# A new form for the state update, a later place for the routing's ranks, and new priorities

## The chip, the cores and the metric

The program runs on one core of a Trainium2 chip. The core has TensorE (PE, with its weight loads PEld), VectorE (DVE), ScalarE (ACT) and GpSimd (POOL); SyncE (SP) issues most DMAs. Each engine works through its own instructions in the order in which the program holds them, and waits on semaphores for the others. The metric is the device time of one execution. Before the change it is 979.59 us, the median of three runs (979.5 to 981.68).

## The reference

Three layers follow each other over 3072 tokens of 384 numbers.

```python
# 1. delta rule, 4 batches x 8 heads, 768 steps, head_dim 48
for t in range(S):
    y[:, :, t] = einsum('bhd,bhde->bhe', q[:, :, t], state)
    v_old = einsum('bhde,bhd->bhe', state, kt)
    state = state + bt[...] * einsum('bhd,bhe->bhde', kt, vt - v_old)
# 2. gated dense layer, 384 -> 1536 -> 384
x = ((x @ w_a) * (x @ w_b)) @ w_out
# 3. eight experts, one for each token, 384 -> 1024 -> 384
e_idx = argmax(x @ w_gate + modality_bias[modality_id], axis=1)
out[mask] = gate_w[mask, None] * (maximum(x[mask] @ w1[e], 0) @ w2[e])
```

## The kernel before

**Number format.** A product of float32 operands is made of float16 pieces: each operand is split into a high half and the low rest, and three matmuls add hi*hi, hi*lo and lo*hi into one region of PSUM. So nearly every operand has a copy by ACT (hi) and a subtraction by DVE or POOL (lo).

**Delta rule.** The 768 steps are cut into 6 chunks of 128. A group g = 4*c + b is chunk c of batch b; there are 24. Within a chunk a triangular system is solved on DVE (L648, L653) and by block products (m1 to m4); from one chunk to the next a state of 48 x 48 per head is carried. For a group, s1_mm takes the state into the right-hand side, s2_mm applies the inverse, s3_mm makes the output and s4_mm the new state: 8 heads, three matmuls each, hi*hi, hi*lo and lo*hi, with 48 key columns as weight and the result on 48 partitions of one PSUM tile, at 0 for an even b and at 64 for an odd one (L905 to L909). s4_f (L915) adds it to the state in float32, s4_hi and s4_lo split that again for the next chunk. The keys' tile t1 holds for a head the hi half in columns 0 to 47 and the lo half in 64 to 111 of 128, with padding between; 20 groups have a state update (the last chunk needs none).

**Dense layer.** The tokens go in tiles t of 256 (the first one in two halves, t = -2 and -1), each in 12 steps m over the 1536 hidden columns: f_mm (18 matmuls into pab, L362 to L364), f_a (ACT copies a), f_ab (DVE multiplies by b), f_hi (ACT, the hi half of g), f_lo (L384, the lo half of g, on DVE or POOL), o_mm (L395 to L397, three matmuls for each half tile into po). Two steps behind f_mm comes o_mm. There are two buffers a, freed by f_lo, and five buffers g.

**Routing.** When the 12 steps of tile t are done, the two PSUM banks po of the tile hold 256 rows of output with 8 logits. r_lg (DVE, L416 to L422) takes logits, argmax and one-hot rows oh; r_mx (DVE, L429) reads both banks for a row maximum; r_hi (ACT, L438) and r_lo (DVE, L444) split the rows; r_rk (PE, L461 to L465) multiplies the one-hot rows by a triangle of ones and writes each token's rank among its expert's tokens into a spare corner of the tile's first bank; r_po (DVE) turns it into a position, and r_sc (POOL) scatters the rows there. setup_routing (L167 to L192) makes the constants for this once, on POOL: it fills a zero tile z, writes pads with it, loads the modality numbers md and builds the bias.

**Experts.** z_cal (DVE, L1158 to L1245) works out which 128-row slots belong to which expert; for each slot h_mm makes pH (L1290 to L1292), DVE subtracts hl (L1303), g_mm and a scatter follow. The first slots' work stands among the last dense steps.

**Order.** Every step is declared with do(f, args, engine, cost, priority, after, take): the steps it comes after and the buffers it takes and who frees them. emit() (L213) then plays a list scheduler: on each engine it takes, among the steps that could start within PATIENCE of the earliest, the one with the least start + HURRY x priority, and it writes the program in the order of its model's starts. The table TUNE adds a number to each priority, by step name and phase of the program; the table ENGINE says where a step runs. Semaphores come from the reads and writes of the tiles: what the planner doesn't know, the engine still waits for on the chip. r_rk is such a case: it is declared after r_lg alone, but the program makes it wait for the other readers of its bank.

## Time and profile before

| | |
|---|---|
| Median of three runs | 979.59 us |
| Profiled execution | 978.26 us, span 976.5, mean granted clock 0.943 |
| PE busy | 879.6 us, 12156 matmuls |
| DVE, ACT, POOL busy | 716.9, 540.4, 281.7 us |
| DMA | 163.57 MB, 167 GB/s |

The span is the stretch from the first to the last instruction that the profile holds; the profiled execution's own time is 1.8 us longer. Busy time is what an engine spends in instructions; for PE it is a union of overlapping matmuls, so that the number of starts per microsecond says more than a row's length. In a row of a timeline the first number is the start, the second the length, and the brackets at its end hold the idle time ahead of it and what ended it. The granted clock is a share of full speed.

### The profile page before, as it was taken

To read this page: it belongs to the slowest core of one execution; us is meant where nothing else is said; L and a number is where in the kernel's file an instruction comes from. 1 tells how busy PE (TensorE), PEld (TensorE's weight loads), DVE (VectorE), ACT (ScalarE), POOL (GpSimd) and SP (SyncE) were. 2 spreads that over 40 slices of the span, in tenths; PEclk is the share of its full clock that TensorE was granted. 3 is DMA by queue.
4 is the path that set the end of the run, shared out by engine and by line. 5 is a ranking of instruction groups with operands and counts; after the bars stand their busy time and mean duration, and the time that the engine had idled before them with its cause. 6 is when DMAs were issued, how large, how long until landed. Compare 5 with 4: busy or idle time off the path is not lost. (4 is left out here: it accounts for less than half of the span.)

```text
span 976.5 us, 30822 instructions
## 1 busy us (share of the span) xinstructions
PE 879.6 (90%) x12156; PEld 704.0 (72%) x12156; DVE 716.9 (73%) x1751; ACT 540.4 (55%) x1072; POOL 281.7 (29%) x409
## 2 busy tenths in 40 slices
PE   3665568999999999999999999999999799999996
PEld 1433367888778887878788887788787677777774
DVE  7889787857997799679975888545877955555551
ACT  4543465547655565555755564555566745555551
POOL 4521015223331233212430422021134423333331
PEclk9676569999999999999999999999999999999998
DMA  7896688674669483864775543331588987999980
GB/s 206 247 245 185 167 175 208 140 181 78 143 150 202 78 130 102 183 152 88 146 173 122 114 88 100 61 64 35 167 249 218 336 256 234 260 264 261 257 218 19
DMA packets 266498, 163.57 MB, mean 167 GB/s; under 512 B 188221, under 2 KB 245357, under 8 KB 266352
## 3 DMA queue, kind: packets, MB, share of 16 engines
q1 hardware_dynamic: 262720, 150.27, 63.9%
q0 software_dynamic: 3632, 11.29, 3.4%
q8 instruction: 100, 1.64, 0.7%
q14 instruction: 46, 0.38, 0.1%
HBM read 97.10 MB, written 30.31 MB: 130 GB/s over the span
## 5 line engine op out<-in xcount | busy, mean ns | idle before, releaser
L332 DVE SCALAR_TENSOR_TENSOR w1l<-w1f,w1h 128x1024 f16<-128x1024 f32 x69 | 80.7, 1220 | 67.2 <-ACT w1h L329 59.5
L362 PE MATMUL pab<-xt,wa 128*128 128x256 f16 (+1 forms) x468 | 122.5, 267 | 2.7 <-DVE a L374 1.3
L364 PE MATMUL pab<-xt,wa 128*128 128x256 f16 (+1 forms) x468 | 122.4, 266 | 0.0
L363 PE MATMUL pab<-xt,wa 128*128 128x256 f16 (+1 forms) x468 | 122.4, 266 | 0.0
L362 PE MATMUL pab<-xt,wb 128*128 128x256 f16 (+1 forms) x468 | 122.3, 266 | 0.0
L363 PE MATMUL pab<-xt,wb 128*128 128x256 f16 (+1 forms) x468 | 122.3, 266 | 0.0
L364 PE MATMUL pab<-xt,wb 128*128 128x256 f16 (+1 forms) x468 | 122.2, 266 | 0.0
L374 DVE SCALAR_TENSOR_TENSOR a<-pab,a 128x256 f32<-128x256 f32 (+1 forms) x156 | 62.2, 400 | 70.0 <-ACT a L329 68.4
L329 ACT ACTIVATE a<-pab 128x256 f32<-128x256 f32 (+1 forms) x156 | 56.5, 364 | 94.2 <-PE pab L364 82.8
L397 PE MATMUL po<-wo,g 128*128 128x392 f16 x288 | 94.8, 329 | 1.7 <-POOL g L384 1.7
L395 PE MATMUL po<-wo,g 128*128 128x392 f16 x288 | 95.1, 330 | 0.0
L396 PE MATMUL po<-wo,g 128*128 128x392 f16 x288 | 94.7, 329 | 0.0
L1290 PE MATMUL pH<-xg_t,w1h 128*128 128x128 f16 x504 | 85.4, 219 | 4.0 <-DMA xg_t<-w2f 3.8
L1292 PE MATMUL pH<-xg_t,w1l 128*128 128x128 f16 x504 | 85.4, 219 | 0.0
L1291 PE MATMUL pH<-xg_t,w1h 128*128 128x128 f16 x504 | 85.4, 219 | 0.0
L329 ACT ACTIVATE g<-a 128x256 f16<-128x256 f32 (+1 forms) x156 | 61.3, 395 | 41.6 <-DVE a L374 32.3
L329 ACT ACTIVATE w1h<-w1f 128x1024 f16<-128x1024 f32 x69 | 68.5, 1047 | 3.7 <-DMA w1f<-in_moe_w_dram 3.2
L648 DVE TENSOR_TENSOR tmp<-A,T 128x31 f32<-128x31 f32 (+15 forms) x186 | 68.4, 368 | 1.5
L653 DVE TENSOR_TENSOR T<-T,tmp 128x31 f32<-128x31 f32 (+15 forms) x186 | 66.3, 357 | 1.7
L762 POOL TENSOR_TENSOR tl<-ttf,th 128x1024 f16<-128x1024 f32 x19 | 42.8, 2256 | 83.7 <-ACT th L329 82.2
L1313 PE MATMUL po<-w2h,hh 128*128 x200 | 65.2, 326 | 1.3 <-ACT hh L1297 0.8
L1315 PE MATMUL po<-w2h,hl 128*128 x200 | 65.2, 326 | 0.0
(301 smaller groups left out, 2863.2 us busy)
## 6 DMA issues: line engine op xcount, KB each, us to landing
w1f<-in_moe_w_dram SPq DMA_DIRECT2D x69, 512.0 KB
w2f<-in_moe_w_dram SPq DMA_DIRECT2D x32, 384.0 KB
gsc<-gs SPq DMA_DIRECT2D x22, 512.0 KB
bq<-aq SPq DMA_DIRECT2D x48, 128.0 KB
bk<-ak SPq DMA_DIRECT2D x40, 128.0 KB
qt<-in_q_dram SPq DMA_DIRECT2D x24, 192.0 KB
kt<-in_k_dram SPq DMA_DIRECT2D x24, 192.0 KB
raw<-in_moe_w_a_dram SPq DMA_DIRECT2D x12, 384.0 KB
```

The source lines that it names most:

```text
L329: S_.activation(out=out, in_=in_, func=ACTF.Copy, scale=scale)
L332: V.scalar_tensor_tensor(out=out, in0=in_, scalar=scale, in1=hi, op0=ALU.mult, op1=ALU.subtract)
L362: T_.matmul(out=p[:, i], lhsT=wa[i][0][:, kk, sl], rhs=xt[:, kk], start=(kk == 0), stop=False)
L363: T_.matmul(out=p[:, i], lhsT=wa[i][0][:, kk, sl], rhs=xt[:, KD + kk], start=False, stop=False)
L364: T_.matmul(out=p[:, i], lhsT=wa[i][1][:, kk, sl], rhs=xt[:, kk], start=False, stop=(kk == KD - 1))
L395: T_.matmul(out=po, lhsT=g[:, 0, sl], rhs=wo[0][:, m], start=(m == 0), stop=False)
L396: T_.matmul(out=po, lhsT=g[:, 0, sl], rhs=wo[1][:, m], start=False, stop=False)
L397: T_.matmul(out=po, lhsT=g[:, 1, sl], rhs=wo[0][:, m], start=False, stop=(m == KF - 1))
L648: V.tensor_tensor(out=LN[c, 2], in0=A[:, j + 1 : 32, j : j + 1].to_broadcast([128, n, w]), in1=T[:, j : j + 1, 0:w].to_broadcast([128, n, ...
L1290: T_.matmul(out=pH[:, u], lhsT=wh[kk][:, sl], rhs=xt[:, kk], start=(kk == 0), stop=False)
L1291: T_.matmul(out=pH[:, u], lhsT=wh[kk][:, sl], rhs=xt[:, KD + kk], start=False, stop=False)
L1292: T_.matmul(out=pH[:, u], lhsT=wl[kk][:, sl], rhs=xt[:, kk], start=False, stop=(kk == KD - 1))
```

## The change

It has four parts.

1. r_rk writes into the second bank of its tile instead of the first; for the last tile (t = 11) it has a tile of its own. The planner now holds r_rk back until r_mx, r_hi and r_lo of that bank are planned.
2. s4_mm takes all 128 columns of a head's keys (hi, padding, lo) as one weight, and multiplies it by uh and by ul: two matmuls per head instead of three. The result has the hi keys' part on partitions 0 to 47 and the lo keys' part on 64 to 111, so a second addition, s4_g, adds the second part to the state behind s4_f. (The lo*lo product is in the sum now.)
3. All numbers of TUNE, PATIENCE and HURRY are new; one line of TUNE is shown.
4. In ENGINE, f_lo goes to POOL in phase 4 (tiles 2 to 10) and to DVE in phase 9; s4_lo goes to DVE everywhere; some a_sq go to POOL, some a_ev, a_lo and p_lo to DVE, c_g2 and x_ev to ACT.

```diff
-    "f_lo:4": 264.09, "f_lo:9": -565.7, "f_mm:3": 234.1, "f_mm:4": 7667.22, "f_mm:9": -249.21, "g_ev:9": -77.5, "g_mm:9": -155.1, "g_sc:9": 43.1,
+    "f_lo:4": -0.4463, "f_lo:9": 310.7308, "f_mm:3": 941.7648, "f_mm:4": 6328.6844, "f_mm:9": 425.6198, "g_ev:9": -1393.6713, "g_mm:9": 1749.0876,
...
-    "c_lo:3": "DVE", "f_lo:3": "POOL", "f_lo:4": "DVE", "f_lo:9": "POOL", "k_pad:0": "DVE", "k_pad:1": "POOL", "m_lo:1": "DVE", "m_lo:2": "POOL",
+    "c_lo:3": "DVE", "f_lo:3": "POOL", "f_lo:4": "POOL", "f_lo:9": "DVE", "k_pad:0": "DVE", "k_pad:1": "POOL", "m_lo:1": "DVE", "m_lo:2": "POOL",
...
-        R["pr"] = pr = PO[2 * t][:, WO : WO + 3 * E].rearrange("p (i e) -> p i e", e=E)
+        if t == NG // 2 - 1:
+            pr = ps_ab.tile([128, 3 * E], F32, name="pr", tag="ab")
+        else:
+            pr = PO[2 * t + 1][:, WO : WO + 3 * E]
+        R["pr"] = pr = pr.rearrange("p (i e) -> p i e", e=E)
...
-        o = 64 * (b % 2)
         for h in range(H):
-            T_.matmul(out=pS[o : o + 48, h], lhsT=t1[:, h, 0, 0:D], rhs=uh[:, h], start=True, stop=False)
-            T_.matmul(out=pS[o : o + 48, h], lhsT=t1[:, h, 0, 0:D], rhs=ul[:, h], start=False, stop=False)
-            T_.matmul(out=pS[o : o + 48, h], lhsT=t1[:, h, 1, 0:D], rhs=uh[:, h], start=False, stop=True)
+            for u in (uh, ul):
+                T_.matmul(out=pS[:, h], lhsT=t1[:, h].rearrange("p t d -> p (t d)"), rhs=u[:, h], start=(u is uh), stop=(u is ul))
...
-        o = 64 * (b % 2)
-        V.scalar_tensor_tensor(out=Sf[b], in0=PS.pop((g, 4))[o : o + 48], scalar=2.0**-6, in1=Sf[b], op0=ALU.mult, op1=ALU.add)
+        V.scalar_tensor_tensor(out=Sf[b], in0=PS[g, 4][0:48], scalar=2.0**-6, in1=Sf[b], op0=ALU.mult, op1=ALU.add)
+
+    def s4_g(g):
+        b = g % B
+        V.scalar_tensor_tensor(out=Sf[b], in0=PS.pop((g, 4))[64:112], scalar=2.0**-6, in1=Sf[b], op0=ALU.mult, op1=ALU.add)
...
-            do(s4_hi, (g,), "ACT", 0.41, o + 5.6, after=[(s4_f, g), (s3_mm, g)])
+            do(s4_g, (g,), "DVE", 0.47, o + 5.55, after=[(s4_f, g)])
+            do(s4_hi, (g,), "ACT", 0.41, o + 5.6, after=[(s4_g, g), (s3_mm, g)])
...
-        do(r_rk, (t,), "PE", 0.1, o + 0.1, after=[(r_lg, t)])
+        if last:
+            do(r_rk, (t,), "PE", 0.1, o + 0.1, after=[(r_lg, t)], take=[("ps_ab", 2, [(r_po, t)])])
+        else:
+            do(r_rk, (t,), "PE", 0.1, o + 0.4, after=[(r_lg, t), (r_mx, t), (r_hi, gs[1]), (r_lo, gs[1])])
```

PE around the ranks' product of tile 9, before: po_11945 and po_11949 are the tile's two banks, pab_12885 is one dense step's tile of 18 matmuls, oh the one-hot rows.

```order
L397 MATMUL po_11949<-wo0_89,g_12817 128x392
L362 LDWEIGHTS wa0_85
L362 MATMUL pab_12885<-xt_12184,wa0_85 128x256
...
L364 MATMUL pab_12885<-xt_12184,wb1_88 128x256
L461 LDWEIGHTS tri_94
L461 MATMUL po_11945<-oh_12908,tri_94 128x8
...
L465 MATMUL po_11945<-oh_12908,ones_95 128x8
L362 LDWEIGHTS wa0_85
```

PE at the same place now: the bank is po_12047, the tile's second one, and pab_12720, pab_12763 and pab_12799 are three dense steps.

```order
L404 MATMUL po_12047<-wo0_89,g_12699 128x392
L369 LDWEIGHTS wa0_85
L369 MATMUL pab_12720<-xt_12038,wa0_85 128x256
...
L369 MATMUL pab_12763<-xt_12038,wa0_85 128x256
...
L369 MATMUL pab_12799<-xt_12038,wa0_85 128x256
...
L371 MATMUL pab_12799<-xt_12038,wb1_88 128x256
L472 LDWEIGHTS tri_94
L472 MATMUL po_12047<-oh_12743,tri_94 128x8
...
L476 MATMUL po_12047<-oh_12743,ones_95 128x8
```

Before, one dense step stands between the tile's last output matmul and the ranks' product; now three do, and the product writes into the bank that the last output matmul wrote.

POOL at the routing's set-up, before (g is what f_lo writes, tri, offc and tok the set-up's constants, pl a step of the delta rule):

```order
L384 TENSOR_TENSOR g<-a,g 128x128 x2
L404 TENSOR_SCALAR sl<-my 128x1
L405 TENSOR_TENSOR sl<-sl 128x1
L384 TENSOR_TENSOR g<-a,g 128x128
L169 AFFINE_SELECT tri<-ones 128x128
L170 IOTA iota_97 128x8
...
L192 TENSOR_TENSOR bias<-bias,bt 128x192
L384 TENSOR_TENSOR g<-a,g 128x128 x2
L807 TENSOR_TENSOR pl<-pm,ph 128x512
```

POOL there now (sq is a step that squares keys for a later chunk):

```order
L391 TENSOR_TENSOR g<-a,g 128x128 x2
L411 TENSOR_SCALAR sl<-my 128x1
L412 TENSOR_TENSOR sl<-sl 128x1
L391 TENSOR_TENSOR g<-a,g 128x128 x2
L818 TENSOR_TENSOR pl<-pm,ph 128x512
L391 TENSOR_TENSOR g<-a,g 128x128 x2
L176 AFFINE_SELECT tri<-ones 128x128
...
L199 TENSOR_TENSOR bias<-bias,bt 128x192
L545 TENSOR_TENSOR sq<-kt 128x384
L391 TENSOR_TENSOR g<-a,g 128x128 x2
```

Three f_lo's stood ahead of the set-up, and two directly behind it; now six stand ahead, and a squaring stands between it and the seventh. On PE, c_g3 of the last weight tile, which frees the set-up's buffer, has moved from ahead of the fourth dense step of the first half tile to ahead of the ninth.

DVE at the handover to the experts, before (hl belongs to the experts' first slots, pi is r_po's last, cn to nu are z_cal, w1l and w2l corrections of expert weights):

```order
L444 SCALAR_TENSOR_TENSOR row<-po,io,row 128x384 x2
L1303 SCALAR_TENSOR_TENSOR hl<-pH,hh 128x512 x2
...
L477 CAST pi<-pf 128x2
L332 SCALAR_TENSOR_TENSOR w2l<-w2f,w2h 128x768
L1158 TENSOR_TENSOR cn_14276<-off,offc 1x8
...
L1245 CAST nu<-cum_14283 1x1
L332 SCALAR_TENSOR_TENSOR w1l<-w1f,w1h 128x1024 x5
L1303 SCALAR_TENSOR_TENSOR hl<-pH,hh 128x512 x2
L332 SCALAR_TENSOR_TENSOR w2l<-w2f,w2h 128x768 x2
```

DVE there now:

```order
L488 CAST pi<-pf 128x2
L451 SCALAR_TENSOR_TENSOR row<-po,io,row 128x384
L1170 TENSOR_TENSOR cn_14022<-off,offc 1x8
...
L1257 CAST nu<-cum_14029 1x1
L1315 SCALAR_TENSOR_TENSOR hl<-pH,hh 128x512 x2
L339 SCALAR_TENSOR_TENSOR w1l<-w1f,w1h 128x1024 x2
L451 SCALAR_TENSOR_TENSOR row<-po,io,row 128x384
L339 SCALAR_TENSOR_TENSOR w1l<-w1f,w1h 128x1024
L339 SCALAR_TENSOR_TENSOR w2l<-w2f,w2h 128x768
L1315 SCALAR_TENSOR_TENSOR hl<-pH,hh 128x512
```

r_po and z_cal have moved ahead of the first two hl and of one r_lo; behind z_cal the first hl come at once, and three w1l and w2l corrections, not five, and one r_lo stand ahead of the next one.

## Rows read from the trace of the kernel before

**Rows 1.** the page's first part: busy us and share of the span.
```profile
PE 879.6 (90%) x12156; PEld 704.0 (72%) x12156; DVE 716.9 (73%) x1751; ACT 540.4 (55%) x1072; POOL 281.7 (29%) x409
```

**Rows 2.** windows: stretch, length, busy us by engine, granted clock, DMA share, GB/s.
```profile
0.00:175.00 175.00, 108.02 (x1287) 78.86 (x1288) 142.57 (x348) 88.22 (x185) 51.74 (x84) 0.72 0.81 203
175.00:750.00 575.00, 564.82 (x8446) 462.80 (x8444) 445.99 (x1226) 336.66 (x732) 162.30 (x249) 1.00 0.58 130
750.00:775.00 25.00, 18.58 (x218) 15.02 (x217) 23.66 (x66) 17.37 (x25) 8.87 (x11) 0.94 1.00 308
```

**Rows 3.** PE's timeline at a state update; its loads before 175 us.
```profile
237.26 0.18 PE L879 MATMUL py<-uh,pl 128*128 128x48 f16 x1
237.38 0.20 PE L907 MATMUL pS<-uh,t1k 128*48 128x48 f16 x1
...
237.98 0.18 PE L909 MATMUL pS<-uh,t1k 128*48 128x48 f16 x1
238.09 0.34 PE L395 MATMUL po<-wo,g 128*128 128x392 f16 x1
...
L907 PEld LDWEIGHTS <-t1k x16: 99/108/130, 138.4 to 159.7; 128*48 128x48 f16 x16
```

**Rows 4.** PE's timeline, the state's first product and a dense step.
```profile
242.63 0.20 PE L822 MATMUL pk<-sst,ak 128*128 128x48 f16 x1
...
243.04 0.27 PE L362 MATMUL pab<-xt,wa 128*128 128x256 f16 x1
243.15 0.27 PE L363 MATMUL pab<-xt,wa 128*128 128x256 f16 x1
```

**Rows 5.** groups of DVE: the addition to the state (count, busy us, mean ns).
```profile
L915 DVE SCALAR_TENSOR_TENSOR sf<-pS,sf 48x384 f32<-48x384 f32 x20 | 11.0, 550 | 0.5
```

**Rows 6.** groups by shape: f_lo on DVE and POOL, its product.
```profile
L384 DVE TENSOR_TENSOR g<-a,g 128x256 f16<-128x256 f32 x104 | 44.4, 428 | 14.4 <-ACT g L329 14.2
L384 POOL TENSOR_TENSOR g<-a,g 128x256 f16<-128x256 f32 x28 | 23.3, 837 | 45.5 <-ACT g L329 45.4
...
L397 PE MATMUL po<-wo,g 128*128 128x392 f16 x288 | 94.8, 329 | 1.7 <-POOL g L384 1.7
```

**Rows 7.** group of PE: the ranks' product, idle before it, releasers.
```profile
L461 PE MATMUL po<-oh,tri 128*128 128x8 f16 x12 | 2.0, 167 | 6.8 <-DVE mo L429 4.3 <-DVE row L444 1.2 <-DVE oh L422 1.1
```

**Rows 8.** timeline of DVE behind the last output product, routing.
```profile
753.92 0.23 DVE L416 SCALAR_TENSOR_TENSOR lg<-po,sl,bias 128x8 f32<-128x8 f32 x1 [0.27 <-PE po L397]
...
757.85 1.14 DVE L444 SCALAR_TENSOR_TENSOR row<-po,io,row 128x384 f16<-128x384 f32 x2
```

**Rows 9.** timeline of POOL, the routing's set-up.
```profile
152.82 0.42 POOL L175 MEMSET z<- 128x386 f32 x1
...
165.31 0.59 POOL L192 TENSOR_TENSOR bias<-bias,bt 128x192 f32<-128x192 f32 x1
```

**Rows 10.** windows of 4 us around the set-up (columns as in rows 2).
```profile
156.00:160.00 4.00, 2.61 (x57) 2.28 (x54) 2.97 (x7) 3.40 (x9) 0.56 (x2) 1.00 1.03 340
164.00:168.00 4.00, 2.33 (x28) 1.62 (x26) 0.80 (x3) 2.02 (x5) 3.70 (x6) 1.00 1.07 219
168.00:172.00 4.00, 4.00 (x39) 3.69 (x37) 3.54 (x7) 2.31 (x7) 1.54 (x2) 0.51 0.36 67
```

**Rows 11.** timeline of ACT, its stall at 129 us.
```profile
129.07 0.55 ACT L329 ACTIVATE wa<-raw 128x384 f16<-128x384 f32 x1 [5.16 <-DVE raw L963]
```

**Rows 12.** handover: timeline of DVE, then what PE waited for, 740 to 800.
```profile
758.90 1.28 DVE L1303 SCALAR_TENSOR_TENSOR hl<-pH,hh 128x512 f16<-128x512 f32 x2
...
761.73 0.15 DVE L1158 TENSOR_TENSOR cn<-off,offc 1x8 f32<-1x8 f32 x1
...
766.43 5.74 DVE L332 SCALAR_TENSOR_TENSOR w1l<-w1f,w1h 128x1024 f16<-128x1024 f32 x5
...
PE pH L1290 <- DVE hl L1303: 5.0, 2, 4.2
```

**Rows 13.** waits of POOL, 240 to 740 us (total, times, longest).
```profile
POOL nm L449 <- DVE mx L418: 59.0, 5, 23.0
```

More of the change, by code (lines that the diff above doesn't have):

```diff
@@ L25 @@
 TUNE = {
[53 rows of a table removed]
[60 rows of a table added]
 }
 PHASE = 25.3
-PATIENCE = ({'PE': 0.7054, 'ACT': 0.1823, 'DVE': 0.06, 'POOL': 0.0334, 'SP': 0.0142}, {'PE': 0.0192, 'ACT': 0.0784, 'DVE': 0.0625, 'POOL': 0.1252, 'SP': 0.6242})
-HURRY = ({'PE': 0.0067, 'ACT': 0.1015, 'DVE': 0.1386, 'POOL': 0.9737, 'SP': 0.0345}, {'PE': 0.7037, 'ACT': 4.3321, 'DVE': 0.2391, 'POOL': 0.9527, 'SP': 0.8016})
+PATIENCE = ({'PE': 0.1441423, 'ACT': 0.0531199, 'DVE': 0.0137721, 'POOL': 2.8466535, 'SP': 0.0044223}, {'PE': 0.0382268, 'ACT': 0.0401974, 'DVE': 0.0662866, 'POOL': 0.0645055, 'SP': 0.8143324})
+HURRY = ({'PE': 0.2337259, 'ACT': 3.7188375, 'DVE': 0.2014005, 'POOL': 0.7865635, 'SP': 1.4968712}, {'PE': 0.0884019, 'ACT': 0.0543269, 'DVE': 0.0452602, 'POOL': 0.1058564, 'SP': 0.0275992})
 WLEAD = 14.0
@@ L1433 @@
         if c < C - 1:
-            do(s4_mm, (g,), "PE", 0.6, o + 5.2, after=[(s2_lo, g), (s3_mm, g)], take=[("pss", 2, [(s4_f, g)])])
+            do(s4_mm, (g,), "PE", 0.4, o + 5.2, after=[(s2_lo, g), (s3_mm, g)], take=[("pss", 2, [(s4_f, g), (s4_g, g)])])
             do(s4_f, (g,), "DVE", 0.47, o + 5.5, after=[(s4_mm, g)] + ([(k_st, b)] if c == 0 else []) + ([(k_st, b - 1)] if c == 0 and b % 2 else []))
-            do(s4_hi, (g,), "ACT", 0.41, o + 5.6, after=[(s4_f, g), (s3_mm, g)])
+            do(s4_g, (g,), "DVE", 0.47, o + 5.55, after=[(s4_f, g)])
+            do(s4_hi, (g,), "ACT", 0.41, o + 5.6, after=[(s4_g, g), (s3_mm, g)])
             do(s4_lo, (g,), "POOL", 0.87, o + 5.7, after=[(s4_hi, g)])
```

121 rows, old and new, of tables (ENGINE, TUNE) are left out of this document.

## The prediction

> **What bounds the kernel now.** I read the page first, for the engine that is never idle. PE is busy 879.6 of 976.5 us [rows 1], so 97 us of idle PE is all that a change of order can win; more needs less work on PE. The windows say where that idle time lies [rows 2]: 67 us in the first 175 us, 10.2 in the 575 us behind them, 6.4 in the 25 us from 750 to 775, and the other 13 in the experts' 200 us and their tail. At the start no engine is full and DVE comes nearest (142.6 of 175): the start is a web of waits, with the granted clock at 0.72 on average. From 175 us on the granted clock is 1.00, PE is 98% busy, and DVE, ACT and POOL all have slack. So there are three kinds of place: the middle, where a microsecond less on PE is a microsecond gained; the handover at 750, where the routing's last steps hold PE; and the start, where what counts is who waits for whom. The chain of waits says nothing here (two pieces of the last write).
>
> The sum is made against the profiled execution, 978.26 us, 1.3 below the median of 979.59. Both are the same program, so I take the difference over to the median.
>
> **1. The state update: -7.2 us.** Twenty groups of 24 matmuls become twenty of 16. I read the price in starts, because the 0.18 us that a row shows is depth, not pitch. The last matmul ahead of a group starts at 237.26, the group's first at 237.38, its last at 237.98, the next product at 238.09 [rows 3]: 0.83 us from start to start, of which 0.60 is 24 matmuls at some 0.025, and the rest the way into the 128*48 shape (0.12) and out of it (0.11), where neighbours of one shape start 0.025 apart (0.60 / 24). The new group has the form of the state's first product, 16 matmuls of a 128*128 shape and 48 columns, two to a weight: 242.63 to 243.04, 0.41 us [rows 4]; with 0.025 for the entry, 0.43. So a group saves 0.40 us. Two of the twenty lie before 175 us, where PE waits anyway (16 of its first line, eight to a group [rows 3]), so 18 count: 7.2. Bounds: 8.0 if all twenty count; 3.6 if only the eight matmuls go (18 x 8 x 0.025) and the shape change isn't what costs the 0.2. I take 7.2, since the gaps stand at both ends of the group and at none inside.
>
> The Trainium skill says in "TensorEngine Tiling (Array Packing)", Key Properties, that changing the tiling mode drains the engine; the trace agrees, with the 0.12 and 0.11 us above, and the change takes that drain away wherever the neighbours are 128*128. Its page "TensorE: Matmul & The Clock Gate", section LDWEIGHTS, speaks against the change: a load takes as long as it has columns (P / 1.2 ns, an estimate of 40 ns for 48 and 107 ns for 128). The trace differs: pairs with 128-column weights also start 0.025 us apart [rows 4].
>
> The second addition on DVE (s4_g) costs 20 x 0.55 = 11 us of DVE [rows 5]. DVE is busy 446 of 575 us in the middle [rows 2], and the 90 subtractions f_lo that leave it take 90 x 0.43 = 38 us away [rows 6]. I cost it at nothing; if its cover is gone, it is up to 0.55 us later per group on the way to the next chunk's state, which is needed many microseconds later.
>
> **2. The wait at the ranks' product: -5.5 us.** PE stood idle 6.8 us in all at its 12 first matmuls, mostly until the row maximum was read from the same bank [rows 7]. The order after an output product is on DVE: the second logits are taken at 753.92, and r_lo's two end at 757.85 + 1.14 = 758.99 [rows 8], so a product that waits for the last reader is free 5 us after the output. In the order before, one step of 18 matmuls of 0.11 us, 2 us [rows 4], was often all that stood between; now three such steps stand there for the tile that I show, and for the others 4 to 16 us by the same count. Only t = 10 has less than 5 us (36 matmuls, 4 us), so I leave 1.2 there and take 6.8 - 1.2 = 5.6, rounded to 5.5. For the last t the product has a bank of its own and only needs the one-hot rows. Bounds: 6.8 (all of it goes) and 2 (DVE is late by another 2 us in half of the places, since all four steps of DVE and ACT must now be over). What is late next is r_po: 45 to 157 rows of PE lie between the ranks' product and the next output product, so it is covered.
>
> **3. f_lo of the middle on POOL: 0.** 90 subtractions go from DVE to POOL, at 0.84 instead of 0.43 us each [rows 6]. Each stands between ACT's copy g and the third matmul of an output product; 90 x 0.41 = 37 us is what it would cost if nothing lay between, 0 if the product always comes later. The trace bears out the second: 28 of the wide ones were on POOL already, and of all 288 rows of that matmul only one waited for POOL, 1.7 us in the start [rows 6]. POOL is busy 162 of 575 us [rows 2], so 75 us more fit. I take 0, with 0 to +17 as the range (below).
>
> **4. The routing's set-up on POOL: +4 us.** From its first MEMSET to its last addition setup_routing holds POOL from 152.82 to 165.31 + 0.59 = 165.9, 13.1 us [rows 9], a wait for its own load included; that MEMSET writes a staging buffer, which comes free with c_g3 of the last weight tile, on PE. In the new order that PE step comes some 12 us of PE's work later and six f_lo's stand ahead of the set-up, so it runs from about 165 to 179, and one a_sq and the seventh f_lo are queued behind it. PE has about 9 us of steps between c_g3 and the output product that needs the seventh, by the order and the pitches above: two f_mm of half width (1 us each), five o_mm of half width (0.5, scaled by columns), s2, s3 and s4 (24, 40 and 16 matmuls of 0.025, 2 us) and six short ones (2 to 3). The set-up takes 13.1 and the two behind it over 1: a wait of 5 to 6. Before, PE stood idle 4 - 2.61 = 1.39 us around 158 and 1.67 around 166, with the set-up on POOL, and then the granted clock was 0.51, the lower of its two levels (1.2 of 2.4 GHz), for 4 us [rows 10]. The half clock may come again behind the new wait, or not. So +2.5 by the waits alone, +6 with a longer stretch of half clock; DVE's longer queue before the first tiles adds up to 3, and ACT's stall of 5.16 us that ends at 129 us [rows 11] partly goes, since the new order has m4_a ahead. I take +4, between 0 and +9.
>
> **5. The handover: -0.8 us.** After the last output product PE waits 25 - 18.58 = 6.4 us [rows 2], 4.2 of it for the subtraction hl, which DVE does behind z_cal (from 761.73, 4.7 us) and five weight corrections of 5.74 us together [rows 12]. Now one r_lo, two hl and one correction of w2 no longer stand ahead of z_cal, which ends some 2.8 us earlier (0.57 + 1.28 + almost 1), but the first two hl come behind it: they end at 766.4 - 2.8 + 1.3 = 764.9 instead of 760.2, so PE waits some 5 us there. The second pair has three corrections ahead of it, not five, and the 4.2 is mostly gone. In all 6.4 becomes some 5.6. Bounds: -3, and +3.4 if the weight corrections moved behind them make the fourth or fifth slot late.
>
> **The sum.** -7.2 - 5.5 + 0 + 4 - 0.8 = -9.5 us: 968.8 against the profiled execution, 970 against the median.
>
> **Rivals.**
> *A. The start takes it all back.* Term 4 at its upper end, +9, with term 2 at 4 and term 1 at 6: -6 - 4 + 9 - 0.8 = -1.8, so 978, give or take 2. For it: the start holds 67 of 97 us of idle time and every wait there has lowered the clock. Against it: the same stretch had waits before, and ACT's stall shortens.
> *B. POOL becomes the late one (slower).* f_lo shares POOL's strict order with r_nm, which waited 59 us for DVE in five places [rows 13], and with indirect writes. Where one of these stands ahead of an f_lo, the buffer a isn't freed, the next products have no place to go, and PE stops. From 1.4 us per tile over nine tiles (12.6 us), with term 4 at +6, the gain is gone: -7.2 - 5.5 + 12.6 + 6 - 0.8 = +5, 985. For it: POOL waited for DVE in these rows before. Against it: 28 f_lo's caused no wait there, and five buffers g lie between.
> *C. The change doesn't do what it says.* The shape change costs nothing by itself and the ranks wait on, because DVE is as late as before: -3.6 - 2 + 4 - 0.8 = -2.4, 977. Against it: rows 3 and the moved rows.
> *D. The wide weight is paid.* If a pair cost the 0.1 us that one load lasts [rows 3], a group of 16 would take 1.6 us and not 0.43, 0.77 more than the group before (0.83): 20 x 0.77 - 5.5 + 4 - 0.8 = +13, 993. Against it: the pitch in rows 4. The rule of the skill named above would have this sign.
>
> **How the numbers follow.** The forecast (964 to 975) has 0.55, A 0.16, B 0.13, C 0.08, D 0.02, and 0.06 is for a start that gets shorter, 955 to 963. What a measurement can tell from no change is 0.3%, 2.9 us: below 976.7 and above 982.5. Faster: 0.55 + 0.06 + a quarter of A and a third of C, 0.68. Slower: B, D and an eighth of A, 0.17. The rest is 0.15. The range leaves out half of B, D and the best starts: 961 to 984.
>
> **What would show it.** Term 1: the state update's groups at x160 with two lines' worth of matmuls, 0.41 us from first start to the next one, shape 128*128. Term 2: idle ahead of the ranks' product under 1.5 us. Term 3: no new wait of PE for POOL in 175 to 750, whose busy sum falls by some 5 us. Term 4: POOL's set-up ending near 180, and PE waiting 5 us for g there; I am wrong if 175 us of the old start become more than 184. Term 5: 750 to 775 with one long wait instead of the last one. If PE is idle in the middle for over 15 us, B is true.

## The result, and the profile after

The changed kernel takes 989.07 us (median), the kernel before 979.55 beside it: a ratio of 1.008, with a 95% interval from 1.0053 to 1.0106, so 0.8% or 9.5 us slower. Forecast were 970, and 961 to 984 as the range. The profiled execution took 988.83 us with a span of 986.7, against 978.26 and 976.5. Of all executions behind the ratios below one is left out, which took 1752 us where the eleven others of its kernel took 978 to 985.

The page's first part and the windows of [rows 1, 2], of the changed kernel (columns as there):

```profile
PE 874.6 (89%) x11996; PEld 700.9 (71%) x11996; DVE 718.9 (73%) x1687; ACT 544.6 (55%) x1072; POOL 330.2 (33%) x493
```

```profile
0.00:175.00 175.00, 106.27 (x1336) 79.78 (x1336) 148.82 (x364) 92.98 (x188) 48.53 (x74) 0.76 0.81 203
175.00:750.00 575.00, 559.62 (x8245) 456.86 (x8246) 439.62 (x1144) 333.97 (x725) 219.42 (x343) 1.00 0.57 128
750.00:775.00 25.00, 18.64 (x214) 15.95 (x213) 21.56 (x63) 14.84 (x21) 4.89 (x10) 0.86 0.88 305
```

PE has 5 us less to do, and its busy time from 175 to 750 us fell by those 5 us, 564.8 to 559.6, as I had asked for. But they became idle time: idle PE in these 575 us went from 10.2 to 15.4 us. DVE did not become free either (446.0 to 439.6): the second addition came, and the steps of the triangular system became longer. Groups of the changed kernel by shape (count, busy us, mean ns, idle ahead), and then two groups of the triangular system, from the page before (L648, L653) and from the page now (L659, L664):

```profile
L472 PE MATMUL po<-oh,tri 128*128 128x8 f16 x11 | 1.9, 171 | 2.7 <-DVE row L451 2.7
L472 PE MATMUL pr<-oh,tri 128*128 128x8 f16 x1 | 0.2, 169 | 0.0
...
L923 DVE SCALAR_TENSOR_TENSOR sf<-pS,sf 48x384 f32<-48x384 f32 x20 | 10.9, 546 | 1.1 <-PE pS L918 0.7
L927 DVE SCALAR_TENSOR_TENSOR sf<-pS,sf 48x384 f32<-48x384 f32 x20 | 11.2, 560 | 0.6
...
L391 POOL TENSOR_TENSOR g<-a,g 128x256 f16<-128x256 f32 x118 | 89.0, 756 | 197.4 <-ACT g L336 195.3 <-DVE iy L358 1.5
```

```profile
L648 DVE TENSOR_TENSOR tmp<-A,T 128x31 f32<-128x31 f32 (+15 forms) x186 | 68.4, 368 | 1.5
L653 DVE TENSOR_TENSOR T<-T,tmp 128x31 f32<-128x31 f32 (+15 forms) x186 | 66.3, 357 | 1.7
```

```profile
L659 DVE TENSOR_TENSOR tmp<-A,T 128x31 f32<-128x31 f32 (+15 forms) x186 | 81.9, 440 | 2.7
L664 DVE TENSOR_TENSOR T<-T,tmp 128x31 f32<-128x31 f32 (+15 forms) x186 | 73.9, 397 | 2.7
```

For the group of [rows 3] term 1 is exact: the timeline now reads 0.02 us into the group and 0.02 out of it, 0.42 us in all instead of 0.83. Not every group has neighbours of the same shape: where a 32*32 or 64*64 product stands beside it, some 0.5 to 0.6 us remain.

```profile
238.39 0.18 PE L890 MATMUL py<-uh,pl 128*128 128x48 f16 x1
238.41 0.18 PE L918 MATMUL pS<-uh,t1k 128*128 128x48 f16 x1
...
238.79 0.18 PE L918 MATMUL pS<-ul,t1k 128*128 128x48 f16 x1
238.81 0.33 PE L402 MATMUL po<-wo,g 128*128 128x392 f16 x1
```

Of term 2, 4.1 us are there: 2.7 us of idle time against the 6.8 of [rows 7]. What came in its place in the middle, among PE's waits from 200 to 752 us (us in total, times, longest):

```profile
PE py L886 <- DVE ul L339: 4.2, 6, 1.4
PE po L472 <- DVE row L451: 2.7, 2, 2.5
PE pab L369 <- DVE a L381: 2.6, 4, 1.8
```

The first is the low half ul that s3_mm needs, the second the ranks' product, the third the buffer pab that f_ab frees. In the same stretch before they stood at 2.2, 6.0 and 0.2.

Then the experts. The first expert product starts at 752.1 us, 1.6 us earlier than before (753.7), and from there this execution loses all that it loses. Windows from the first product of expert slot 0 to that of slot 8, and on to slot 24, before and then after:

```profile
753.70:822.60 68.90, 62.15 (x751) 50.09 (x749) 48.49 (x91) 38.96 (x53) 22.46 (x25) 0.98 0.87 278
822.60:955.40 132.80, 128.73 (x1536) 101.44 (x1537) 75.12 (x80) 71.92 (x96) 41.64 (x48) 1.00 0.90 247
```

```profile
752.10:831.30 79.20, 65.30 (x750) 53.07 (x749) 53.30 (x96) 42.59 (x58) 17.68 (x25) 0.94 0.88 272
831.30:966.30 135.00, 129.27 (x1539) 101.41 (x1537) 75.25 (x80) 72.08 (x96) 41.64 (x48) 1.00 0.88 237
```

Eight slots take 79.2 us instead of 68.9. Of the 10.3 us, 7.1 are idle PE (13.9 us, 6.8 before) and 3.1 longer busy time, at a granted clock of 0.94 instead of 0.98: it stands at the lower of its two levels, 0.50, from 760.9 to 767.7 us and from 822.4 to 825.8, beside the two long waits below, and before the change only from 772.2 to 775.6. From slot 8 on the pace is the same within 2%: 135.0 and 132.8 us. PE's waits in the 79 us, and the stretch of DVE that answers to [rows 12] (xg_t are a slot's tokens; their rows are fetched into w2f, the four staging buffers that the second weights use too, and transposed from there):

```profile
PE pH L1302 <- DVE hl L1315: 6.3, 2, 5.7
PE pH L1302 <- DMA xg_t<-w2f: 4.3, 1, 4.3
PE po L1326 <- DVE w2l L339: 2.3, 2, 1.6
```

```profile
756.65 0.14 DVE L1170 TENSOR_TENSOR cn<-off,offc 1x8 f32<-1x8 f32 x1
...
761.31 0.13 DVE L1257 CAST nu<-cum 1x1 int32<-1x1 f32 x1
761.37 1.26 DVE L1315 SCALAR_TENSOR_TENSOR hl<-pH,hh 128x512 f16<-128x512 f32 x2
```

The counting z_cal (cn to nu, 756.65 to 761.44) now stands ahead of hl, as the order said, and PE waits 5.7 us for hl. 4.3 us come at 821.8 us, where slot 7 waits for its tokens, and 2.3 for corrections of the second weights (w2l). On DVE 21 of these corrections now stand ahead of the last tile's routing; before the change 26 did. On SP seven of the 32 loads of second weights, 384 KB each, are issued behind the first expert product, the last at 800.0 us; before the change two were, the last at 761.9. By the windows 272 x 79.2 = 21.5 MB instead of 278 x 68.9 = 19.2 MB are moved beside these slots (GB/s by us), and those five loads are 2.0 of the 2.3 MB. In the 50 us ahead, DMA had time for them: its share was 0.69 from 700 to 725 us and 0.65 from there to the first product, against 0.90 and 0.74 before.

### The profile page after: what moved, and what is told of

It reads as the page before. It is cut to its first block, busy times and chain, and to the rows that moved or that the text cites. A ratio compares the mean times of both kernels' runs of the same rounds, so it can differ in the third digit from the quotient of the medians.

```text
span 986.7 us, 30518 instructions
## 1 busy us (share of the span) xinstructions
PE 874.6 (89%) x11996; PEld 700.9 (71%) x11996; DVE 718.9 (73%) x1687; ACT 544.6 (55%) x1072; POOL 330.2 (33%) x493
## 5 line engine op out<-in xcount | busy, mean ns | idle before, releaser
L391 POOL TENSOR_TENSOR g<-a,g 128x256 f16<-128x256 f32 (+1 forms) x142 | 100.8, 712 | 219.9 <-ACT g L336 217.8
L381 DVE SCALAR_TENSOR_TENSOR a<-pab,a 128x256 f32<-128x256 f32 (+1 forms) x156 | 62.1, 400 | 71.3 <-ACT a L336 70.4
L1302 PE MATMUL pH<-xg_t,w1h 128*128 128x128 f16 x504 | 87.0, 221 | 9.5 <-DMA xg_t<-w2f 9.4
L1303 PE MATMUL pH<-xg_t,w1h 128*128 128x128 f16 x504 | 87.0, 221 | 0.0
L659 DVE TENSOR_TENSOR tmp<-A,T 128x31 f32<-128x31 f32 (+15 forms) x186 | 81.9, 440 | 2.7
L664 DVE TENSOR_TENSOR T<-T,tmp 128x31 f32<-128x31 f32 (+15 forms) x186 | 73.9, 397 | 2.7
L1326 PE MATMUL po<-w2l,hh 128*128 x200 | 65.1, 326 | 2.3 <-DVE w2l L339 2.3
```

The source lines that it names most:

```text
L391: eng_of(f_lo, t, m).tensor_tensor(out=g[:, 1], in0=FA.pop((t, m)), in1=g[:, 0], op=ALU.subtract)
L659: V.tensor_tensor(out=LN[c, 2], in0=A[:, j + 1 : 32, j : j + 1].to_broadcast([128, n, w]), in1=T[:, j : j + 1, 0:w].to_broadcast([128, n, ...
L1302: T_.matmul(out=pH[:, u], lhsT=wh[kk][:, sl], rhs=xt[:, kk], start=(kk == 0), stop=False)
L1303: T_.matmul(out=pH[:, u], lhsT=wh[kk][:, sl], rhs=xt[:, KD + kk], start=False, stop=False)
```

## The experiments

Ratios are against the kernel before, run beside them on the same chip, with their 95% intervals.

**One part at a time.** The state product of the change in the kernel before, in an order that is the same instruction by instruction but for it:

```diff
-            T_.matmul(out=pS[o : o + 48, h], lhsT=t1[:, h, 0, 0:D], rhs=uh[:, h], start=True, stop=False)
...
+            for u in (uh, ul):
+                T_.matmul(out=pS[:, h], lhsT=t1[:, h].rearrange("p t d -> p (t d)"), rhs=u[:, h], start=(u is uh), stop=(u is ul))
...
+        for o in (0, 64):
+            V.scalar_tensor_tensor(out=Sf[b], in0=pS[o : o + 48], scalar=2.0**-6, in1=Sf[b], op0=ALU.mult, op1=ALU.add)
```

> The kernel before with the new state update alone: two matmuls per head, 128 key columns as one weight, and the second addition directly behind the first on DVE. Every step stands where it stood. Theory (the form saves what I read from the starts, and the loss comes from elsewhere): 7 us faster than before, 972 to 974, the group 0.43 us from start to start and no new wait. Rival 1 (only the eight matmuls go, the shape change costs nothing): 3.6 us faster. Rival 2 (the saving is used up by the second addition, which makes the next state late): no change, with new waits ahead of the state's first product.

Measured: 988.78 us against 980.77, 1.0091 (1.0061 to 1.012), 8 us slower, worse than the theory and both rivals. A group between 128*128 products saves its 0.40 us, the mean of the 18 behind 175 us 0.35 (0.86 to 0.50). PE's idle time from 200 us to the first expert product grows by more, from 10.0 to 19.7 us. Its waits from 200 to 764 us, of which the first two were 4.3 and 2.2 us before:

```profile
PE po L461 <- DVE mo L429: 5.9, 8, 1.9
PE py L875 <- DVE ul L332: 4.9, 4, 1.6
PE pu L853 <- POOL tl L762: 1.2, 1, 1.2
```

So the term of 7.2 us is a loss when it stands alone. Its two sides were then taken apart. The new form without the second addition (`for o in (0,)`):

> The kernel before with the new state update's 16 matmuls, and without the second addition: the lo keys' part of the product is computed and left out of the state. Every step stands where it stood. Theory (the second addition on DVE, 20 x 0.55 us, is what made the new form slower, because DVE's order in the middle has no slack where PE waits for it): 6 to 8 us faster than the kernel before, 972 to 975. Rival (the wide weight or the result on 112 partitions costs something itself): no faster than before, 980 or more.

Measured: 981.48 us, 1.0007 (0.9982 to 1.0032). Seven us less on PE bring nothing that can be told from noise: PE is idle for 14.9 us from 175 to 750 us instead of 10.2. The rival (the wide weight costs something itself) has no support, since the groups are as short as with the second addition, 0.50 us in the mean. And the kernel before with a second, idle addition on DVE, 20 x 0.55 us:

```diff
+        for s in (2.0**-6, 0.0):
+            V.scalar_tensor_tensor(out=Sf[b], in0=pS, scalar=s, in1=Sf[b], op0=ALU.mult, op1=ALU.add)
```

> The kernel before with its own state update, and one more addition of the same size on DVE behind s4_f (it adds the same product times zero): 20 x 0.55 us of DVE and nothing else. Theory (DVE has no slack at these places): 11 to 16 us slower than before, 991 to 997, the idle time of PE ahead of py, of po and of the ranks' product grown between 200 and 620 us. Rival (DVE has slack, 78% busy): within 3 us of before.

Measured: 987.74 us, 1.0087 (1.0056 to 1.0118), 6.8 us slower than the 980.91 beside it, for this group of DVE:

```profile
L917 DVE SCALAR_TENSOR_TENSOR sf<-pS,sf 48x384 f32<-48x384 f32 x40 | 22.1, 553 | 1.1
```

So 11 us more on an engine that is busy 446 of 575 us [rows 2] cost 7, between theory and rival. The reverse, with no addition at all:

```diff
-        V.scalar_tensor_tensor(out=Sf[b], in0=PS.pop((g, 4))[o : o + 48], ...)
+        PS.pop((g, 4))
```

> The kernel before, without its 20 state additions (s4_f, 48 x 384, 550 ns each, 11.0 us of VectorE); the state is then not updated, and nothing else is changed, the order included. Theory (VectorE's in-order chain sets the pace of the middle, as the idle addition, +11 us of work for +6.8 us, had it): about 6 to 7 us faster, 973 to 974 against 980. Rival (TensorE sets the pace and the idle addition only pushed VectorE over a brim): no change, within 2 us.

and the same with the 16-matmul form:

> The state product with all 128 columns of the key tile as one weight (16 matmuls for 24, 0.40 us less of TensorE in each of 20 groups) and no state addition at all (11 us less of VectorE); the state is not updated, the order is the one before. Theory (TensorE and VectorE bound the middle together, so that relief of one returns as waits on the other): clearly more than without the additions alone, some 10 to 14 us faster than before. If VectorE alone set the pace: the same as without the additions alone, 6 to 7 us. If TensorE alone: 7 to 8 us here and nothing without the additions alone.

Both totals (1040.68 and 1035.87 us) say nothing, since without the state other tokens go to other experts and there are more slots (31 instead of 25). Up to the first expert product the programs can be compared: it starts at 752.2 and 751.1 us, against 753.7, and at 762.1 with the idle addition. Part of such a difference is the start, which varies by itself. So I count from the last matmul of the first tile's dense steps (202.9 us before) to the first expert product: 550.9 us before, 551.3 and 553.2 in two more profiles of the same order up to there; 550.4 with 7 us less on PE, 549.3 with 11 us less on DVE, 546.8 with both, 557.7 with 11 us more on DVE. The theory that DVE sets the pace fell with this, and so did that of PE; without the additions the next state does not even wait for its product. Both reliefs together give 4 to 6 us of 18, one idle addition costs 4 to 7 of 11. My reading, which no run shows directly: the order is one in which each wait is just met; work that is added makes it miss, work that is taken away leaves the next engine's step where it was.

**The ranks' product alone**, moved ahead of the last dense step before the next output product, in the second bank, with r_po behind it where that stood earlier:

```diff
+            last = [j for j in range(i, top) if steps[line[j]][0] == "PE" and steps[line[j]][1] > 0.8]
+            i = last[-1] if last else i
+            line.insert(i, rk)
...
+            pr = PO[2 * t + 1][:, WO : WO + 3 * E]
```

> The kernel before with the ranks' product alone moved: into the second bank (a tile of its own for the last t), and on PE to the place ahead of the last dense step before the next tile's first output product; where the position r_po stood ahead of it on DVE it follows it. All else stands where it stood. Theory: PE's idle time ahead of this product falls from 6.8 to 1 to 2.7 us, and the time by 4 to 5.5 us, 974 to 976. Rival (the wait only moves on to the next output product, which needs r_po): idle time appears there, and the time falls by less than 2 us.

Measured: 984.53 us, 1.0033 (1.0009 to 1.0057). PE's idle time there falls only from 6.8 to 4.8 us, and DVE, which must read the ranks, now waits 3.3 us for them in 8 places (0.4 before). Theory and rival both missed.

**f_lo on POOL alone**, the 104 wide ones of the middle, at their old places:

```diff
+        e = P_ if phase(12 * t + m + 0.4) == "4" else eng_of(f_lo, t, m)
```

> The kernel before with 104 of its subtractions f_lo (those of phase 4) given to POOL, each at the place in the program where it stood on DVE; all else as before. Theory (POOL's f_lo slow DVE's own multiplications of the triangular solve down, L648 and L653, by some 20 us in all, and take 0.41 us longer each, so that DVE's relief of 44 us is worth less than it looks): these two groups rise from 368 and 357 to 400 to 440 ns, and the time stays within 4 us of before. Rival 1 (DVE is what PE waits for, so the relief counts): 4 to 8 us faster. Rival 2 (POOL's strict order makes f_lo late): over 5 us slower, with PE waiting for g of POOL.

Measured: 993.05 us, 1.0133 (1.01 to 1.0167), 12 us slower, as the second rival had it. It shows two prices. DVE's two groups of the triangular system (page) go from 368 and 357 ns to 404 and 414, 17 us of the 44 that f_lo had taken:

```profile
L654 DVE TENSOR_TENSOR T<-T,tmp 128x31 f32<-128x31 f32 (+15 forms) x186 | 76.9, 414 | 2.4
L649 DVE TENSOR_TENSOR tmp<-A,T 128x31 f32<-128x31 f32 (+15 forms) x186 | 75.2, 404 | 2.2
```

And PE waits for g, which in the profile before it did once [rows 6]:

```profile
PE po L398 <- POOL g L385: 6.1, 8, 2.8
```

The longest of these, 2.78 us at 619.5, is followed by 1.6 us more, because the granted clock falls behind it (0.60 and 0.55 in the means of two windows, so mostly at 1.2 GHz, the lower of its two levels, and not at 2.4), in windows of 2 and 4 us:

```profile
616.00:620.00 4.00, 1.22 (x9) 0.52 (x7) 0.87 (x2) 0.83 (x2) 2.15 (x3) 1.00 0.52 112
620.00:622.00 2.00, 2.00 (x12) 1.42 (x11) 0.00 (x0) 0.00 (x0) 0.05 (x1) 0.60 0.73 158
622.00:624.00 2.00, 2.00 (x12) 1.36 (x10) 0.00 (x0) 0.00 (x0) 0.00 (x0) 0.55 0.55 132
624.00:626.00 2.00, 2.00 (x18) 1.54 (x17) 0.42 (x1) 0.80 (x2) 0.59 (x1) 1.00 0.45 70
```

**Code and tables.** The old code with all new tables, and the new code with all old ones:

> The code of the kernel before with the new tables: the priorities, the patience and the choice between VectorE and GpSimd for f_lo. Theory: the move of the f_lo to GpSimd alone cost 12 us in the old order; the new priorities were made for it, so that some of this comes back, 982 to 990. Rival (the new priorities are what costs the experts 12 us): 990 to 995, with the correction of the second weights late at the hand-over as in the changed kernel.

> The changed code (state product, second addition, later rank product) with the old tables, f_lo mostly on VectorE. Theory: the state form alone cost 8.0 us, the rank product alone 3.2 us; together about 11 us slower than before, 989 to 993, which is no better than the changed kernel (989.1). Rival (the new tables are the loss): 975 to 982, faster than the changed kernel.

Measured: 1009.32 us, 1.0298 (1.0266 to 1.0329), and 1002.6, 1.0231 (1.0196 to 1.0267), both worse than foreseen. Code and tables belong together: with the tables of the other, each loses 23 or 29 us, and the new tables win back some 14 of the 23 that the new code costs in an order made for the old one.

**The hand-over.** Two tries to give the second weights of the changed kernel their old numbers back, all three (w_ld, w_hi, w_lo) or w_lo alone:

```diff
-    "w_ld:9": 656.8088, "w_hi:9": -53.4954, "w_lo:9": 1827.4899
+    "w_ld:9": 272.48, "w_hi:9": -75.69, "w_lo:9": 718.7
```

> The changed kernel with three numbers of its priorities set back to those of before: those of the w2 loads (w_ld), their copies (w_hi) and corrections (w_lo). By the order all 32 loads then stand ahead of the expert's w1 loads on SP, as 30 of them did before; in the changed kernel 7 stand among and behind them. Nothing moves ahead of the last two dense tiles. Theory (the seven late w2 loads are what makes the experts late, 10 of the 12 us lost behind 753 us): 8 to 11 us faster than the changed kernel, 978 to 981, the waits of PE for xg_t and w2l near 800 to 825 gone. Rival (the loss is the first two hl behind z_cal, and the rest follows): under 3 us faster.

> The changed kernel with one number of its priorities set back, that of w_lo, the corrections of the w2 weights: by the order 29 instead of 25 of the 32 w2 loads then stand ahead of the first w1 load of the experts, all 32 ahead of the last rows' transposes, and nothing moves ahead of the last dense tile. Theory (late w2 loads cost the experts some 4 to 6 of the 12 us): 3 to 6 us faster than the changed kernel, 983 to 986. Rival (the experts' loss is in the handover's hl and z_cal): the same as the changed kernel, 988 to 990.

Measured: 1003.95 us, 1.0231 (1.0192 to 1.0271), and 1001.62, 1.0242 (1.0201 to 1.0284); both expectations missed by their sign. Neither edit was as small as it was meant: the planner moved other steps with it, and the first expert product itself came later (765.6 and 759.4 us). In the first the experts' own first weights (w1e) were late, in the other four corrections (3.5 us) stood ahead of f_ab in DVE's queue. PE's waits from 740 to 860 and from 700 to 860 us:

```profile
PE pH L1296 <- DVE w1e L331: 16.4, 4, 12.3
```

```profile
PE pH L1294 <- DMA xg_t<-w2f: 12.4, 3, 10.6
PE pH L1294 <- DVE hl L1307: 7.7, 2, 6.0
PE pab L361 <- DVE a L373: 5.3, 1, 5.3
```

The reverse, the kernel before with its last loads of second weights held behind loads of w1:

```diff
+ {25: [(e_w1, 4, 1)], 26: [(e_w1, 5, 2)], 27: [(e_tr, 4)], 28: [(e_tr, 6)]}.get(j, [])
```

> The kernel before with the w2 loads 25 to 31 held back on SP behind expert w1 loads and the rows' transposes, as in the changed kernel; all else is unchanged up to the last output product. Theory (late w2 loads): 7 to 11 us slower than before, 986 to 990, with PE waiting for xg_t and w2l between 790 and 830. Rival (they are harmless, the loss is the handover's order on DVE): within 2 us of before.

Measured: 984.05 us, 1.0042 (1.0018 to 1.0066), between theory and rival. Seven loads are now issued behind the first expert product, as in the changed kernel, and the first eight slots take 74.4 us instead of 68.9. The 5.0 us wait for hl [rows 12] is gone, because DVE's order changed too, and a wait for the tokens takes its place (750 to 860 us):

```profile
PE pH L1290 <- DMA xg_t<-w2f: 10.6, 4, 7.6
```

Then single waits in the changed kernel. hl ahead of z_cal, nothing else:

```diff
+        line.remove((z_cal,))
+        line.insert(line.index((h_lo, 0, 1)) + 1, (z_cal,))
```

> The changed kernel with one difference of order: VectorE computes the corrections of the first hidden block (hl) ahead of the counting that lays out the experts' slots, as before the change, and not behind it. Theory (the 5.7 us wait of TensorE for hl at 762 us is one part of the 12 us that the experts lost): the copies hh end at 758.0 and 759.2, so hl comes 2 to 3 us earlier and the counting 3 us later; 2 to 3 us faster than the changed kernel, about 986 against 989. Rival (the end is set by the late loads of the second weights and of the tokens): no change, or 1 to 3 us slower because the counting releases the tokens' loads later.

Measured: 989.94 us, 1.0094 (1.0074 to 1.0114), no gain. The hl wait halves and w2l takes it (745 to 860 us):

```profile
PE po L1329 <- DVE w2l L342: 7.6, 3, 5.6
PE pH L1305 <- DMA xg_t<-w2f: 4.3, 2, 3.1
PE pH L1305 <- DVE hl L1318: 3.0, 2, 2.4
```

Half of the last tile's f_lo back on POOL, planned anew:

```diff
+            if name == "f_lo" and args >= (11, 0) and args[1] % 2:
+                new = "POOL"
```

> The changed kernel with the odd half of the last tile's f_lo (6 of 12) on GpSimd instead of VectorE, and the order worked out anew with that: 32 of 32 loads of the second weights stand ahead of the first fetch of tokens, as before the change, instead of 27. Theory (the new assignment puts the last 14 f_lo on VectorE, where the kernel before had them on GpSimd; the corrections of the second weights fall 5 behind, and the ring of 4 buffers holds the loads back): the wait of 4.3 us for tokens at 821 us and the 2.3 us for w2l go, 4 to 7 us faster than the changed kernel, 982 to 985. Rival (the corrections are late because SyncE's queue stood behind the transposes of the experts' first tokens from 704 to 713 us): the same, within 2 us.

Measured: 991.53 us, 1.012 (1.0098 to 1.0141), no gain. All 32 loads stand ahead of the first fetch of tokens and w2l waits 0.8 us. But the loads are hardly earlier: six are still issued behind the first expert product, not two as before the change, so this run does not test early loads. The first eight slots take 78.2 us, with these waits:

```profile
PE pH L1304 <- DMA xg_t<-w2f: 7.4, 4, 5.4
PE pH L1304 <- DVE hl L1317: 6.0, 1, 6.0
```

Each mended wait had another behind it. So the order as a whole was put to the test: the changed kernel up to tile 9, and from there each engine's steps in the order of the kernel before, f_lo on its engines.

```diff
+        line = [k for k in line if k not in {k for e, k in tail}] + [k for e, k in tail]
+        for e, k in tail:
+            steps[k] = (e, *steps[k][1:])
```

> The changed kernel as it is up to the end of the dense layer's tile 9 (about 680 us), and from there every engine's steps in the order, and the f_lo on the engine, of the kernel before. Theory (the 10 us that the first eight expert slots lost come from the new order of the hand-over as a whole: 21 corrections of second weights ahead of the routing instead of 26, and 2.4 MB more of loads left to be done beside the experts): slots 0 to 8 take 69 to 70 us again instead of 79, and the time is 977 to 981. Rival (the experts are longer for the changed state of the buffers and queues when they start, whatever the order of the tail): 985 or more.

Measured: 981.86 us, 1.0006 (0.9985 to 1.0026). The first eight slots (756.7 to 826.9 us):

```profile
756.70:826.90 70.20, 62.94 (x751) 51.17 (x748) 48.92 (x91) 38.74 (x53) 23.53 (x25) 0.95 0.86 268
```

70.2 us instead of 79.2, with two loads behind the first product as before the change. The gap is far beyond the spread: the eight slots took 68.3 to 70.4 us in nine profiles with the old hand-over and the same slots, 78.2 to 79.8 in the three with the new one (the changed kernel and the two tries above). This is the answer to the 9.5 us: they are the new order of the hand-over, with its f_lo on DVE, and all that lies ahead of it, taken together, neither wins nor loses. Last, small mends there, in the kernel before and in this one: the corrections of the second hidden block ahead of two of w1 (and for the kernel before, a bank of its own for the last ranks' product).

```diff
+        mv = [(e_lo, 3, 0), (e_lo, 3, 1)]
...
+        i = line.index((h_lo, 1, 1)) + 1
+        line[i:i] = mv
```

> The kernel before with two small things at the hand-over alone: the last rank product gets a PSUM bank of its own, as in the change, and the corrections of the second hidden block stand ahead of two corrections of w1 on VectorE. Theory: the wait of 4.2 us for hl at 766 to 772 us shrinks by 2 to 3 us, and nothing in the middle is touched: 977 to 978 against 980, the one version that could beat both. Rival: the corrections of w1 that are pushed back are late in their turn, within 1 us of the kernel before.

> The same, and the corrections of the second hidden block ahead of two corrections of w1, as in the kernel before with small mends. Theory: as much better than the kernel with the old tail as there, 0 to 2 us; if the old tail brings the changed kernel to 977 to 980, this is the version that could beat both. Rival: the loads of w1 pace the slots after the eighth (832 to 966 us took 133 to 136 us in every run, at a DMA share of 0.88 to 0.90), so that what the first slots gain is waited for there: no difference.

Measured: 978.38 us, 0.999 (0.9967 to 1.0013), and 981.97, 1.0012 (0.9996 to 1.0029): no difference. In the first, slot 3 starts 3.7 us earlier than before (778.4 against 782.1) and slot 12 only 0.4 (854.9 against 855.3). No version that was tried beats the kernel before by more than its measurement can tell.

## Why the prediction was wrong

Two steps failed. The sum booked 12.7 us of gain in the middle (terms 1 and 2) on the ground that PE's time there is the kernel's time, with the second addition at nothing; the profiles show 3 to 6. And term 5 put the hand-over at -0.8, at most +3.4; it measured +10.3.

**Its first paragraph failed.** "The middle, where a microsecond less on PE is a microsecond gained" was read from 98% busy PE, and the form without the second addition refutes it: 7 us less on PE, 1.0007. A busy share says how little the engine waits in this order, not that the next engine's result will be there earlier. The Trainium skill, "Perfetto Trace Analysis", section Identifying the Most-Contended Engine, has the same rule (optimize the engine of highest occupancy first), with a caution that TensorE's matmul busy share is no good measure of how near it is to its roofline, the best it could do. The runs here go with the caution and not with the rule: at 98% busy, 7 us less work shortened nothing.

**Term 1 (-7.2).** The saving on PE was nearly right, 0.40 us for the group read and 0.35 in the mean of the 18 (6.3 us), and the load of 128 columns costs nothing at this length, so rival D fell. The step that failed is "I cost it at nothing" for the second addition. Its cover, 129 us of idle DVE, is an average; in the places where DVE's queue leads to the ranks' product (mo) and to ul there was too little, as the grown waits there say. Alone it costs 6.8 us, and the new form with it 8.

**Term 2 (-5.5).** 4.1 us of the wait went, not 5.5: 2.7 are left where I had under 1.5. No run shows that the time fell by them. In the old order, alone, the later place is 3 to 4 us slower, with DVE waiting 3.3 us for the ranks. "It is covered", said of r_po, counted PE's rows and not DVE's queue.

**Term 3 (0).** As an edit by itself it costs 12 us, near the price of rival B (12.6), though only in part by its road: PE waits for g 6.1 us in 8 places, and DVE loses 17 us to the overlap. The second was not in my sum. The Trainium skill, "SBUF — State Buffer", section Who interferes with whom, has a rule that speaks against the change and that I had not weighed: a VectorE instruction with two inputs in SBUF contends with a GpSimd instruction that reads SBUF. The trace agrees in direction, with 36 and 57 ns more per step. In the changed order PE waits for POOL hardly at all (0.4 us for tl), so the new tables cover the late g; they don't cover the overlap (440 and 397 ns).

**Term 4 (+4).** This one held better than one profile shows. In the profiled execution the set-up moved as forecast (164.60 to 178.89 us on POOL), but PE did not wait for g: a load (bq) had held it for 3.7 us at 174.9, with the clock at 0.50 behind that. Six other kernels of these experiments have the same start, and in each PE waits for that g at 179 to 184 us, for 2.5 to 7.2 us; four kernels with the old start have such a wait too, of 1.7 to 3.3 us. In the kernel with hl ahead of z_cal (PE's waits from 150 to 206 us):

```profile
PE po L407 <- POOL g L394: 5.0, 1, 5.0
```

The last matmul of the first tile's dense steps starts at 204.5 to 209.2 us in these seven profiles, 206.9 in the mean, and at 202.3 to 202.9 in those four. Of the 4.3 us between the means 0.9 are 16 matmuls, 0.056 us each, that now stand ahead of this mark, so some 3.4 us are lost. The fastest of the seven starts is the one that was profiled for the changed kernel, which is luck.

**The middle as a whole.** From that matmul to the first expert product the profiles agree well: 547.6, 547.6, 547.5 and 547.0 us in four kernels with the new order up to tile 9 (two of them with the old tail behind it), 550.9, 551.3 and 553.2 in three with the old one. So the middle wins 3 to 6 us, the 0.9 of above among them, and not 12.7, and the start loses about as much. The first expert product comes at 752.1, 756.3, 756.7 and 753.1 us and at 753.7, 753.6 and 755.8: means of 754.6 and 754.4. The kernel with the old tail says the same with an interval: 1.0006. So for terms 1 to 4 -8.7 were forecast and 0 measured.

**Term 5 (-0.8, bounds -3 and +3.4).** This is where the time went: +10.3 us by the profile, and some 7 by the medians (989.07 to 981.86). I had the 5 us wait at hl right (5.7), and its gain at the second pair too. What I did not price is that five more loads of second weights, 2.0 MB, move into a stretch whose DMA share is 0.87 already, beside new waits for the tokens (4.3 us at slot 7) and for w2l (2.3), and that the clock falls at two waits there instead of one. Late loads alone, in the old order, cost 3.3 us by the medians and 5.5 in the first eight slots, though a wait of 5.0 us for hl went with them; so they are part of it. I had named it ("if the weight corrections moved behind them make the fourth or fifth slot late") and gave it 3.4 us. Which of the three waits weighs most stays open: half of the hl wait, once mended, came back as one for w2l, no run made the loads early without other moves, and only the whole old order takes the loss away.

**Rivals.** B had the sign and nearly the time (985), but not the place: PE's idle time in the middle is 15.4 us, just over the 15 that I had set as its mark, but only 0.4 of it is for POOL, so the mark does not tell B from what happened. A was right that the start takes something back, 3.4 us, but it came on top of a middle that hardly gained. Its ground that every wait there lowered the clock is too strong: around 158 us PE stood idle for 1.39 us at 1.00 [rows 10].

## What to carry to other kernels

An order written out for given costs is a fit: edit one step in it and price the edit by the queue it lengthens, not by the busiest engine's share; 11 us more on DVE, which has 22% of slack, cost 7 here; 7 us less on PE gave nothing and 11 less on DVE some 2. Where a stretch ahead of another has spare DMA and the next has little (0.58 and 0.87), look at what is still to be loaded when the second begins: five loads that slipped over that border were part of a loss of 7 to 10 us. And compare stretches over several profiles, between marks that stand behind the same work: the same start differed by 4.7 us between seven profiles, the middle behind it by 0.6 between four.

## What the hardware showed unexpectedly

A wait of PE can cost more than its length: 2.78 us of waiting were followed by two windows of 2 us at a mean granted clock of 0.60 and 0.55, and a dense step of 18 matmuls there took 3.59 us instead of 1.97. Steps of the triangular system on DVE slow down by 10 to 16% (368 to 404 ns, 357 to 414 ns) when POOL takes 104 subtractions of f_lo, and in sum by some more in the changed kernel (440 and 397 ns). Weight loads of 128 columns with 48 moving columns cost no more than those of 48: each matmul has its load, which takes 0.096 us with 128 columns and 0.100 with 48, starts stay 0.025 us apart, and without a change of shape the group's way in and out shrinks from 0.23 to 0.04 us.
